# Convolution and gated FFN on one core: turning the last block's second half of results apart, slots 4, 5 and slots 6, 7, for a last transform with zero-padded tables

## Chip, cores and metric

The kernel runs on 1 core of one Trainium2 chip. The metric is the device time of one execution in microseconds (us), the median of several runs. All arithmetic of the part that changes is in fp32.

## What is computed

The input is x of 2048 positions and 512 channels. It is normalised over the channels (xn). One branch convolves every channel of xn with a kernel of 2048 terms that comes from a state-space model (A, B, C, dt, 128 states a channel), by Fourier transforms; the other is a feed-forward network on xn. The result joins both:

```python
y = irfft2(rfft2(up) * rfft2(Kp))[..., :L]     # convolution, L = 2048
s = y + xn * Dskip
h = gelu(xn @ w1 + b1)
g = silu(h @ w2 + b2)
return x + s * g
```

## The kernel before

The first 396 us or so compute the feed-forward network (its gated result goes to HBM) and the convolution kernels, interleaved by an order that is written out by hand. The rest, which the change touches, is the convolution, in `NB` = 4 blocks of 128 channels. The 2048 positions are taken as 32 x 64, so that each Fourier transform has two short steps. Engines: PE is TensorE, DVE VectorE, ACT ScalarE, POOL GpSimd, SP the queue that issues most DMAs. Each engine takes its instructions in the order in which the code issues them; the last part has no planner, so the order of the lines is the order of the work.

A block passes these steps:

- `first_dft` (the 32-step, line 879) of the signal and of the convolution kernel.
- `second_dft` (line 901): the 64-step. The 32 frequencies of the first step are done in eight **slots** of four, g = 0 to 7, as matmuls on 64x64 tiles of the array.
- `spectrum`, `product`, `combine` (lines 915 to 939): ACT copies one factor out of PSUM, DVE multiplies the two spectra and adds the products to `Y`, one tile for two slots.
- `back_dft` (line 941): the inverse of the 64-step for two slots j = 0 to 3 (slots 2j, 2j + 1), into two PSUM banks `sa`, a = 0 and 1, on the upper and the lower 64 rows of the array.
- `back_out` (line 951): copies `sa` to `Z`. `Z` has two tiles, kh = 0 for slots 0 to 3 and kh = 1 for slots 4 to 7; each holds, for each of 64 positions, the 16 frequencies' real and imaginary parts, 32 numbers.
- `turn` (line 964): DVE transposes `Z` in blocks of 32x32 to `T`, in two halves s, so that the 32 numbers come to lie on the partitions.
- `last_dft` (line 982): the inverse of the 32-step. For each of four groups w of output partitions and each of G = 4 groups g of channels, one matmul on a 32x32 tile of the array (row group g, column group w) with the table `gc[:, kh]`. kh = 0 starts the sum in PSUM and kh = 1 finishes it.
- `last_out` and, in the last block, `gated` and `added`: the result is multiplied by the gate, x is added, and `store` sends it to HBM.

An fp32 matmul shows as two passes in the trace, each with a weight load of its own (PEld), so 16 matmuls are 32 records.

In blocks 0 to 2, `two_slots` lays a block's last steps beside the next block's first ones. The last block has `slot` for its eight slots, and behind slot 7 a tail of its own (line 1197 on). There the results of slots 6, 7 (j = 3) are computed in halves h0 and h1, and the outputs in two halves of positions, `py[0]` (in two tiles `wide`) and `py[1]` (four banks). The order of the tail before: back_dft and back_out for h0, then for h1 (bank 0 copied by ACT, bank 1 by DVE); last_dft of kh = 0 on the first half; two transposes `turn(b, 1, s)` of all of kh = 1; four matmuls of an identity matrix on PE, whose result is overwritten; last_dft of kh = 0 on the second half; last_dft of kh = 1 on the first and the second half. Then come `gated` (lines 1223 and 1226) and `added` (line 1230) and four stores. `gated(0, n)` needs the first half of the outputs, `gated(1, n)` the second.

Of the kernel before, what the change touches and what calls it, by code (L numbers as in the profile page):

```python
# [11 lines left out]
F32 = mybir.dt.float32  # L12
# [8 lines left out]
P = 128  # L21
L, D, NS, F = 2048, 512, 128, 1792
G = D // P
NF = F // P
KD = D // P
N1, N2 = 32, 64
NB = 4
# [5 lines left out]
NQ = L // P  # L33
# [95 lines left out]
def _shape_constants():  # L129
    n1 = np.arange(N1)[:, None]  # L130
    k1 = np.arange(N1)[None, :]
    a = 2 * np.pi * n1 * (k1 + 0.25) / N1
    cf = np.zeros((G, N1, 2, 2, N1))
    for g in range(G):
        cf[g, :, g % 2] = np.stack([np.cos(a), -np.sin(a)], 1)
    cg = np.stack([np.cos(a).T, -np.sin(a).T], 1).reshape(2, 2, 4, 2, 2, N1)
    cg = np.tile(cg.transpose(1, 3, 2, 4, 0, 5).reshape(1, N1, 2, N1), (G, 1, 1, 1))
    n2 = np.arange(N2)[:, None]
    k2 = np.arange(N2)[None, :]
    cm = np.zeros((2, N2, N1, 2, N2))  # L140
    ct = np.zeros((2, N2, N1, 2, N2))
    for k in range(N1):
        th = 2 * np.pi * (n2 * (k + 0.25) / L + n2 * k2 / N2)
        c, s = np.cos(th), np.sin(th)
        cm[:, :, k, 0, :] = c
        cm[:, :, k, 1, :] = s
        ct[0, :, k, 0, :] = c.T / L
        ct[1, :, k, 0, :] = -s.T / L
        ct[0, :, k, 1, :] = s.T / L
        ct[1, :, k, 1, :] = c.T / L  # L150
    ct = ct.reshape(2, N2, N1 // 2, 2, 2, N2).transpose(3, 1, 2, 0, 5, 4)
    cb = np.zeros((CH, NPC, CH, NPH))
    for d in range(CH):
        cb[d, :3, d, :N1] = N2 * np.arange(N1)
        cb[d, :3, d, N1:] = np.arange(N2 // 2) + 0.5
        cb[d, 3:, d, :N1] = 1.0
    f = np.float32
    return {
        "cf": cf.reshape(P, 4 * N1).astype(f),
        "cg": cg.reshape(P, 2 * N1).astype(f),  # L160
        "cm": cm.reshape(P, N1 * 2 * N2).astype(f),
        "ct": ct.reshape(P, N1 * P).astype(f),
        "cb": cb.reshape(CH * NPC, CH * NPH).astype(ml_dtypes.bfloat16),
    }
# [3 lines left out]
def kernel(  # L168
# [5 lines left out]
    V, A, GP, PE, SY = nc.vector, nc.scalar, nc.gpsimd, nc.tensor, nc.sync  # L174
# [613 lines left out]
    def open_mid():  # L788
        SB["pm"] = pm = opened(p2, "pm", "right")
        SB["ps"] = opened(pz, "psm", "left", bufs=2, space=PSUM)  # L790
        SB["tcn"] = pm.tile([P, N1, P], F32, name="tcn")
        SB["tb"] = SB["tcn"].rearrange("p (k o) m -> p k o m", o=2)
        xf[1] = pm.tile([P, 2, 2, N1, N2], F32, tag="X1", name="X1")
        SB["uh"] = pm.tile([P, 2, 2, P], F32, tag="uh", name="uh_0_0", bufs=2)
        SB["t0"] = pm.tile([P, 2, 2, 4, N2], F32, tag="t0", name="t0_0_0", bufs=2)
        SB["gc"] = pm.tile([P, 2, N1], F32, name="gc")
        gx[0] = new_tail(0)
        yy[0, "T", 1] = new_turn(0, 1)

# [141 lines left out]
    def back_dft(b, j, es=slice(0, 4)):  # L941
        if (b, j, "p") not in yy:
            yy[b, j, "p"] = [bank(f"sa{b}_{j}_{a}") for a in range(2)]
        for e in range(4)[es]:
            for o in range(2):
                for a, p in enumerate(yy[b, j, "p"]):
                    r = slice(64 * a, 64 * a + 64)
                    PE.matmul(p[:, e, :], yy[b, j][r, o, e, :], SB["tb"][r, 4 * j + e, o, :],  # L948
                              start=(o == 0), stop=(o == 1), skip_group_check=True)

    def back_out(b, j, es=slice(0, 4), engs=(A, A)):
        kh = j // 2
        if (b, "Z", kh) not in yy:
            yy[b, "Z", kh] = SB["pm"].tile([P, N2, N1 // 2, 2], F32, tag=f"Z{kh}", name=f"Z{b}_{kh}")
        for a, (p, eng) in enumerate(zip(yy[b, j, "p"], engs)):
            k = 8 * (j % 2) + 4 * a
            src = p.rearrange("p k (x c) -> p x k c", c=2)[:, :, es]
            dst = yy[b, "Z", kh][:, :, k:k + 4, :][:, :, es]
            eng.copy(dst, src) if eng is A else eng.tensor_copy(dst, src)

    def new_turn(b, kh):
        return SB["pm"].tile([P, 4, 2, 8, N1], F32, tag=f"T{kh}", name=f"T{b}_{kh}")

    def turn(b, kh, s):
        if (b, "T", kh) not in yy:
            yy[b, "T", kh] = new_turn(b, kh)
        Z = yy[b, "Z", kh].rearrange("p (w s q) k c -> p w s q (k c)", w=4, s=2)
        V.transpose(yy[b, "T", kh][:, :, s], Z[:, :, s])

    gx = {}  # L970

# [10 lines left out]
    def last_dft(b, kh, py, q=slice(0, NQ)):  # L982
        T = yy[b, "T", kh].rearrange("p w s q i -> p w (s q) i")
        for w in range(4):
            for g in range(G):
                r, m = slice(g * N1, (g + 1) * N1), slice(w * N1, (w + 1) * N1)
                o = py[g].rearrange("p (q i) -> p q i", i=N1)
                PE.matmul(o[m], SB["gc"][r, kh], T[r, w, q], start=(kh == 0), stop=(kh == 1), skip_group_check=True)  # L988
# [173 lines left out]
    with tc.manual_schedule():  # L1162
        SB["spare"] = False
        open_front()
        z_load(NTB - 1)
        for j in range(4):
            mc_load(j)
        side_skip(0)
        side_turn(1, eng=GP)
        SB["spare"] = True  # L1170
        for p in "S0 F00 S1 S2 F01 S3 L0 F10 L1 A0 F11 A1 L2 L3 A2 A3".split():
            if p[0] == "F":
                k = int(p[1]), int(p[2])
                first_dft(0, *k)
                first_out(0, *k, (A, A, V, V))
                if k[0]:
                    mc_turn(k[1])
                    if k[1] == 0:
                        kernel_load(1)
            elif p[0] == "A":  # L1180
                silu(NTB - 1, int(p[1]))
            else:
                second_part(*steps[-2 if p[0] == "S" else -1], int(p[1]))
                if p[0] == "L":
                    z_add(NTB - 1, int(p[1]))
        z_store(NTB - 1)
        SB["spare"] = False
        fa.close()
        open_mid()
        ct_load(0)  # L1190
        SY.dma_start(SB["gc"].rearrange("p h n -> p (h n)"), cg)
        for b in range(NB - 1):
            for i in range(4):
                two_slots(b, i)
        for g in range(8):
            slot(NB - 1, g)
        b = NB - 1
        h0, h1 = slice(0, 2), slice(2, 4)
        back_dft(b, 3, h0)
        back_out(b, 3, h0)  # L1200
        wide = [SB["ps"].tile([P, 2, 4 * P], F32, tag="ri", name=f"y{b}_{n}", bufs=2) for n in range(2)]
        py = [[wide[g // 2][:, g % 2, :2 * P] for g in range(G)]]
        halves = [slice(0, NQ // 2), slice(NQ // 2, NQ)]
        back_dft(b, 3, h1)
        back_out(b, 3, h1, (A, V))
        last_dft(b, 0, py[0], halves[0])
        py.append([bank(f"y{b}_{g}_1").rearrange("p e m -> p (e m)")[:, :2 * P] for g in range(G)])
        for s in range(2):
            turn(b, 1, s)
        for n in range(4):  # L1210
            PE.matmul(py[1][0][:, :P], ident, ident, start=True, stop=True, skip_group_check=True)
        last_dft(b, 0, py[1], halves[1])
        for s in range(2):
            last_dft(b, 1, py[s], halves[s])
        gt, xt_ = gx[b]
        def parts(s, n):
            return tuple(t[:, halves[s], 64 * n:64 * n + 64] for t in (gt, xt_))

        def gated(s, n):
            if s:  # L1220
                for g in (2 * n, 2 * n + 1):
                    gg = gt[:, halves[1], g * N1:g * N1 + N1]
                    V.tensor_mul(gg, py[1][g].rearrange("p (q i) -> p q i", i=N1), gg)
            else:
                gp = parts(0, n)[0].rearrange("p q (g i) -> p g q i", i=N1)
                V.tensor_mul(gp, wide[n][:, :, :2 * P].rearrange("p g (q i) -> p g q i", i=N1), gp)

        def added(s, n):
            gv, xv = parts(s, n)
            (V if n else GP).tensor_add(xv, gv, xv)  # L1230

        gated(0, 0)
        added(0, 0)
        gated(0, 1)
        gated(1, 0)
        added(0, 1)
        for t in range(2):
            store(b, t, (SY, A)[t % 2])
        gated(1, 1)
        for n in range(2):  # L1240
            added(1, n)
        for t in range(2, 4):
            store(b, t, (SY, A)[t % 2])
# [33 lines left out]
```

## Time and profile before

| | us |
|---|---|
| median of 3 runs | 533.06 (532.49 to 534.91) |
| the profiled execution, its own time | 532.96 |
| its span from first to last instruction | 531.1 |
| PE busy in the span | 516.4 |
| DVE busy | 429.7 |
| ACT busy | 390.8 |
| POOL busy | 260.7 |

The mean granted clock of TensorE was 0.995. Times in the profile run from the span's start. A row of the order of time has start, length, engine, line, operation, what is written from what, and the count; in brackets stands how long the engine was idle before and what ended that. A row of the chain that ended last has start, length, engine, tile and line. A row of a stretch has its bounds and length and then, for each engine, the busy time and the count of instructions in it. PE names the passes, PEld the weight loads.

### The profile page before, as it was taken

Reading aid. Unit: us, or ns where it says so; the run is one execution under the profiler, and the core shown is the slowest. Engines: PE = TensorE matmul, PEld = TensorE weight load, DVE = VectorE, ACT = ScalarE, POOL = GpSimd, SP = SyncE. Lnnn points to the kernel's source line nnn. Section 1 sums busy time; section 2 is a strip of 40 time slices with the busy share of each in tenths; the row PEclk is TensorE's granted clock in tenths of the full one; section 3 lists DMA queues with packets and bytes.
Section 4 is the critical chain, followed back from the end, with each engine's and each line's share of the span. In section 5 each row is a group of like instructions: output and inputs, shape, how many; then the busy total and the mean of one; then the engine's idle time right before and its main releaser. Section 6 shows DMA issues by size and latency. Waiting matters only on the chain.

```text
span 531.1 us, 16527 instructions
## 1 busy us (share of the span) xinstructions
PE 516.4 (97%) x6999; PEld 422.4 (80%) x6999; DVE 429.7 (81%) x726; ACT 390.8 (74%) x556; POOL 260.7 (49%) x384
## 2 busy tenths in 40 slices
PE   8899999999999999999999999999999999999993
PEld 8677787877777777877777787778889998998882
DVE  6989899999998789787875886898257779677896
ACT  3588996999987988888778799799454573663330
POOL 5619478667597569669817175645301002103042
PEclk9999999999999999999999999999999999999998
DMA  7946527762427966418135532591656639542552
GB/s 221 307 121 195 187 94 233 241 199 77 161 80 198 352 215 180 140 29 252 41 108 175 185 59 107 133 176 45 233 209 224 77 102 214 164 166 81 195 193 97
DMA packets 86086, 85.84 MB, mean 162 GB/s; under 512 B 41878, under 2 KB 60698, under 8 KB 84988
## 3 DMA queue, kind: packets, MB, share of 16 engines
q1 hardware_dynamic: 76944, 66.43, 42.3%
q0 software_dynamic: 8768, 17.83, 10.8%
q8 instruction: 55, 0.90, 0.7%
q10 hardware_dynamic: 300, 0.53, 0.3%
q14 instruction: 19, 0.16, 0.1%
HBM read 51.22 MB, written 33.55 MB: 160 GB/s over the span
## 4 chain that ended last, share of the span: by engine, by line
PE 84%; DVE 6%; ACT 3%; POOL 3%; DMA 2%; issue 2%; POOLq 0%; DVEq 0%; ACTq 0%
PE s L911 11%; PE z L287 9%; PE z L289 8%; PE z L288 8%; PE f L248 8%; PE f L250 8%; PE f L249 8%; PE s L889 6%; PE sa L948 6%; PE kg L655 5%; PE ph L591 3%; PE y L988 2%; DMA w1s<-in_B_w_dram 1%; DVE hl L274 1%; PE xT L359 1%
## 5 line engine op out<-in xcount | busy, mean ns | idle before, releaser
L616 POOL TENSOR_TENSOR mm<-mm,rc 128x32 f32<-128x32 f32 (+4 forms) x150 | 97.1, 647 | 11.8
L287 PE MATMUL z<-w2h,hh 128*128 128x512 f32 x224 | 95.6, 427 | 0.0
L248 PE MATMUL f<-xh,w1h 128*128 128x512 f32 x220 | 91.7, 417 | 0.9 <-ACT w1h L231 0.6
L250 PE MATMUL f<-xh,w1l 128*128 128x512 f32 x220 | 87.1, 396 | 2.2 <-DVE w1l L233 1.5
L289 PE MATMUL z<-w2h,hl 128*128 128x512 f32 x224 | 87.7, 392 | 0.1
L288 PE MATMUL z<-w2l,hh 128*128 128x512 f32 x224 | 87.7, 391 | 0.0
L249 PE MATMUL f<-xl,w1h 128*128 128x512 f32 x220 | 86.8, 394 | 0.0
L605 DVE SCALAR_TENSOR_TENSOR ra<-ra,ph 128x512 f32<-128x512 f32 x64 | 43.8, 684 | 19.4 <-ACT ra L599 18.5
L911 PE MATMUL s<-X,mc 64*64 64x128 f32 x1536 | 58.0, 272 | 0.4 <-DVE t L929 0.4
L929 DVE TENSOR_TENSOR t<-s,uh 128x512 f32<-128x512 f32 x64 | 40.9, 684 | 15.1 <-ACT uh L919 11.6
L250 PEld LDWEIGHTS f<-xh,w1l 128*128 128x128 f32 x220 | 41.3, 188 | 12.4 <-DVE w1l L233 2.4
L639 DVE TENSOR_TENSOR e<-mm,ra 128x1024 f32<-128x1024 f32 x32 | 42.7, 1336 | 10.0 <-ACT ra L627 4.2
L248 PEld LDWEIGHTS f<-xh,w1h 128*128 128x128 f32 x220 | 41.5, 189 | 11.4 <-ACT w1h L231 1.1
L262 ACT ACTIVATE f<-f,b1s 128x512 f32<-128x512 f32 x56 | 37.2, 665 | 18.1 <-PE f L250 16.9
L289 PEld LDWEIGHTS z<-w2h,hl 128*128 128x128 f32 x224 | 42.1, 188 | 10.1 <-DVE hl L274 0.5
L613 POOL COPY mm<-rc 128x32 f32<-128x32 f32 x30 | 15.5, 516 | 69.5 <-DVE e L646 39.6
L287 PEld LDWEIGHTS z<-w2h,hh 128*128 128x128 f32 x224 | 42.4, 189 | 8.9 <-issue 0.3
L911 PEld LDWEIGHTS s<-X,mc 64*64 64x64 f32 x1536 | 44.8, 133 | 5.3 <-issue 1.5
L288 PEld LDWEIGHTS z<-w2l,hh 128*128 128x128 f32 x224 | 42.2, 189 | 8.2
L249 PEld LDWEIGHTS f<-xl,w1h 128*128 128x128 f32 x220 | 41.3, 188 | 9.1
L919 ACT COPY uh<-s 128x512 f32<-128x512 f32 x32 | 18.8, 587 | 40.1 <-PE s L911 22.0
L274 DVE TENSOR_TENSOR hl<-f,hh 128x512 fp32r<-128x512 f32 x56 | 37.8, 682 | 10.6 <-ACT hh L268 10.6
(183 smaller groups left out, 1130.9 us busy)
## 6 DMA issues: line engine op xcount, KB each, us to landing
x<-in_A_u_dram SPq DMA_DIRECT2D x8, 512.0 KB
xs<-x SPq DMA_DIRECT2D x8, 512.0 KB
xt_h<-xh POOLq DMA_DIRECT2D x4, 1024.0 KB, 5.7
xt_l<-xl POOLq DMA_DIRECT2D x4, 1024.0 KB, 8.2
kgd<-ko SPq DMA_DIRECT2D x16, 256.0 KB
za<-zo SPq DMA_DIRECT2D x4, 1024.0 KB
xh<-xt_h POOLq DMA_DIRECT2D x4, 1024.0 KB, 6.7
xl<-xt_l POOLq DMA_DIRECT2D x4, 1024.0 KB, 10.0
```

What stands on the lines that cost most here:

```text
L248: PE.matmul(p, wh[:, k, :], xh[:, k, :], start=(k == 0), stop=False)
L249: PE.matmul(p, wh[:, k, :], xl[:, k, :], start=False, stop=False)
L250: PE.matmul(p, wl[:, k, :], xh[:, k, :], start=False, stop=(k == KD - 1))
L274: V.tensor_sub(hl, hf, hh)
L287: PE.matmul(z, hh[:, s], wh, start=(f0 == 0 and not rows), stop=False)
L288: PE.matmul(z, hh[:, s], wl, start=False, stop=False)
L289: PE.matmul(z, hl[:, s], wh, start=False, stop=(f0 == FA - 1))
L605: V.scalar_tensor_tensor(ra[:, 0, c], ra[:, 1, c], MAGIC, p, op0=ALU.subtract, op1=ALU.subtract)
L616: GP.tensor_mul(mv[:, :, 0:3:2, w:2 * w], mv[:, :, 0:3:2, 0:w], rc[:, 2 + 2 * i:4 + 2 * i, :].rearrange("p j c -> p c j").unsqueeze(3).to_ ...
L639: V.tensor_mul(e1, m1.unsqueeze(1).to_broadcast([P, 2, CH, N1]), ra[:, :, :, :N1])
L911: PE.matmul(p[ka * 64:(ka + 1) * 64, r, o, :, jj], w, xf[b][h, c, :, k, :], start=(c == 0), stop=(c == 1), skip_group_check=True)
L929: V.tensor_mul(t, p[:, i, :, 1].unsqueeze(1).to_broadcast([P, 2, 2, P]), uh)
```

## The change

For kh = 1 of the last block, `back_out` writes `Z` in another layout: slots 4, 5 (j = 2, written as j % 2 = 0) fill its first half and slots 6, 7 its second, each with 64 positions by 16 numbers. A 32x32 block of a transpose then holds two neighbouring positions by 16 numbers instead of one by 32. So slots 4, 5 can be transposed (`turn_pairs(b, 0, s)`) before slots 6, 7 are there. After a transpose the partitions hold 16 numbers of the even position and 16 of the odd one. `last_pairs` therefore has two matmuls, e = 0 and e = 1, for each group pair (w, g), with tables whose other 16 rows are zeros, and each gives every second position: 128 columns instead of 256. `gc` grows from 2 to 6 tables of 32 columns.

```diff
+    pair = np.zeros((G, 2, 2, 2, N1 // 2, N1))
+    for j in range(2):
+        for o in range(2):
+            pair[:, j, o, o] = cg[:, N1 // 2 * j:N1 // 2 * (j + 1), 1]
+    pair = pair.reshape(G, 4, N1, N1).transpose(0, 2, 1, 3)
+    cg = np.concatenate([cg, pair], 2)
...
-        SB["gc"] = pm.tile([P, 2, N1], F32, name="gc")
+        SB["gc"] = pm.tile([P, 6, N1], F32, name="gc")
...
-            dst = yy[b, "Z", kh][:, :, k:k + 4, :][:, :, es]
+            if b == NB - 1 and kh:
+                Z = yy[b, "Z", kh].rearrange("p x k c -> p (x k c)").rearrange("p (j x k c) -> p j x k c", j=2, k=N1 // 4, c=2)
+                dst = Z[:, j % 2, :, 4 * a:4 * a + 4, :][:, :, es]
+            else:
+                dst = yy[b, "Z", kh][:, :, k:k + 4, :][:, :, es]
...
+    def turn_pairs(b, j, s):
+        if (b, "T", 1) not in yy:
+            yy[b, "T", 1] = new_turn(b, 1)
+        Z = yy[b, "Z", 1].rearrange("p x k c -> p (x k c)").rearrange("p (j w s q) -> p j w s q", j=2, w=4, s=2)
+        T = yy[b, "T", 1].rearrange("p w s q i -> p (w s q i)").rearrange("p (j s w q) -> p j s w q", j=2, s=2, w=4)
+        V.transpose(T[:, j, s], Z[:, j, :, s])
+
+    def last_pairs(b, j, py, s):
+        T = yy[b, "T", 1].rearrange("p w s q i -> p (w s q i)").rearrange("p (j s w q) -> p j s w q", j=2, s=2, w=4)
+        for w in range(4):
+            for g in range(G):
+                r, m = slice(g * N1, (g + 1) * N1), slice(w * N1, (w + 1) * N1)
+                o = py[g].rearrange("p (q e i) -> p q e i", e=2, i=N1)
+                for e in range(2):
+                    PE.matmul(o[m, :, e], SB["gc"][r, 2 + 2 * j + e], T[r, j, s, w], start=False, stop=(j == 1), skip_group_check=True)
...
         back_dft(b, 3, h0)
         back_out(b, 3, h0)
         wide = [SB["ps"].tile([P, 2, 4 * P], F32, tag="ri", name=f"y{b}_{n}", bufs=2) for n in range(2)]
         py = [[wide[g // 2][:, g % 2, :2 * P] for g in range(G)]]
-        halves = [slice(0, NQ // 2), slice(NQ // 2, NQ)]
+        last_dft(b, 0, py[0], halves[0])
         back_dft(b, 3, h1)
-        back_out(b, 3, h1, (A, V))
-        last_dft(b, 0, py[0], halves[0])
+        for s in range(2):
+            turn_pairs(b, 0, s)
+        back_out(b, 3, h1)
+        last_pairs(b, 0, py[0], 0)
         py.append([bank(f"y{b}_{g}_1").rearrange("p e m -> p (e m)")[:, :2 * P] for g in range(G)])
-        for s in range(2):
-            turn(b, 1, s)
-        for n in range(4):
-            PE.matmul(py[1][0][:, :P], ident, ident, start=True, stop=True, skip_group_check=True)
         last_dft(b, 0, py[1], halves[1])
         for s in range(2):
-            last_dft(b, 1, py[s], halves[s])
+            turn_pairs(b, 1, s)
+        last_pairs(b, 1, py[0], 0)
+        for j in range(2):
+            last_pairs(b, j, py[1], 1)
```

On DVE this is the tail before, from slot 7's last combination on (Y_3, Z_1 and T_1 are the tiles of slots 6, 7 and of kh = 1; T_0 and Z_0 those of kh = 0; y_0, y_1 are the first half of the outputs, y_0_1 and on the second):

```order
L937 TENSOR_TENSOR Y_3_7115<-t_3_6_7111,t_3_6_7112 128x2x128
L968 STREAM_TRANSPOSE T_0_7074<-Z_0_7061 128x4x256
L959 COPY Z_1_7175<-sa_3_1_7184 128x64x4
L968 STREAM_TRANSPOSE T_1_7227<-Z_1_7175 128x4x256 x2
L1226 TENSOR_TENSOR last<-y_0_7195,last 128x2x8x32
L1226 TENSOR_TENSOR last<-y_1_7196,last 128x2x8x32
L1223 TENSOR_TENSOR last<-y_0_1_7223,last 128x8x32
```

And the same place on DVE after the change:

```order
L943 TENSOR_TENSOR Y_3_7115<-t_3_6_7111,t_3_6_7112 128x2x128
L978 STREAM_TRANSPOSE T_0_7074<-Z_0_7061 128x4x256
L985 STREAM_TRANSPOSE T_1_7221<-Z_1_7175 128x512 x4
L1254 TENSOR_TENSOR last<-y_0_7195,last 128x2x8x32
L1254 TENSOR_TENSOR last<-y_1_7196,last 128x2x8x32
L1251 TENSOR_TENSOR last<-y_0_1_7258,last 128x8x32
```

DVE's copy has gone to ACT, and two transposes have become four of half the size, of which the first two read what slots 4, 5 left. On PE, this is the tail before, from back_dft's second half on, each kind of row once:

```order
L948 MATMUL sa_3_1_7184<-tcn,Y_3_7115 128x128
L988 MATMUL y_0_7195<-T_0_7074,gc 32x256 x2
...
L1211 MATMUL y_0_1_7223<-ident 128x128 x4
L988 MATMUL y_0_1_7223<-T_0_7074,gc 32x256
...
L988 MATMUL y_0_7195<-T_1_7227,gc 32x256 x2
...
L988 MATMUL y_0_1_7223<-T_1_7227,gc 32x256
```

And on PE after the change (in a row of 32x4x32 the four matmuls are e = 0, 1 of two channel groups, in one of 32x4x32 x2 they are e = 0, 1 of one):

```order
L1014 MATMUL y_0_7195<-T_0_7074,gc 32x256 x2
...
L954 MATMUL sa_3_1_7184<-tcn,Y_3_7115 128x128
L994 MATMUL y_0_7195<-T_1_7221,gc 32x4x32 x4
...
L1014 MATMUL y_0_1_7258<-T_0_7074,gc 32x256
...
L994 MATMUL y_0_7195<-T_1_7221,gc 32x4x32 x4
...
L994 MATMUL y_0_1_7258<-T_1_7221,gc 32x4x32 x2
```

The first half's last_dft has moved ahead of back_dft's second half, the identity matmuls are gone, and each of the two calls that read T_1 has become two calls of twice as many matmuls.

More of the change, by code (lines that the diff above doesn't have):

```diff
@@ L159, in _shape_constants @@
         "cf": cf.reshape(P, 4 * N1).astype(f),
-        "cg": cg.reshape(P, 2 * N1).astype(f),
+        "cg": cg.reshape(P, 6 * N1).astype(f),
         "cm": cm.reshape(P, N1 * 2 * N2).astype(f),
@@ L1198 @@
         h0, h1 = slice(0, 2), slice(2, 4)
+        halves = [slice(0, NQ // 2), slice(NQ // 2, NQ)]
         back_dft(b, 3, h0)
```

## The prediction

> **What bounds the kernel now.** I read the page first, then the chain that ended last from 505 us on, then the rows of the engines in order of time for the last 15 us. On the page TensorE (PE) is busy for nearly the whole span. The other three lines serve later: all instructions, and the bytes that two instruction queues fetched.
>
> ```profile
> span 531.1 us, 16527 instructions
> PE 516.4 (97%) x6999; PEld 422.4 (80%) x6999; DVE 429.7 (81%) x726; ACT 390.8 (74%) x556; POOL 260.7 (49%) x384
> ...
> q8 instruction: 55, 0.90, 0.7%
> q14 instruction: 19, 0.16, 0.1%
> ```
>
> That share says nothing of the place of the change, which lies behind slot 7 of the last block. The chain there (start, length, work) changes hands:
>
> ```profile
> 511.10 3.65 PE s L911 x128
> 514.75 2.04 PE sa L948 x32
> 516.78 1.34 ACT Z L959 x3
> 518.12 0.04 issue
> 518.17 1.43 PE sa L948 x16
> 519.60 0.64 PE y L988 x32
> 520.24 1.09 PE y L1211 x8
> 521.33 1.41 PE y L988 x59
> 522.74 0.02 issue
> 522.76 0.12 DVE last L1226
> ...
> 523.97 0.18 DVE last L1223
> ```
>
> The reader is to see that PE hands over to VectorE (DVE) at 522.76, and that DVE then carries it. What stands on both engines, and on ScalarE (ACT), in that time:
>
> ```profile
> 516.76 1.63 ACT L959 COPY Z<-sa 128x512 f32<-128x512 f32 x4 [1.32 <-PE sa L948]
> 517.73 1.24 DVE L968 STREAM_TRANSPOSE T<-Z 128x1024 f32<-128x1024 f32 x1
> 518.17 1.43 PE L948 MATMUL sa<-tcn,Y 64*128 64x128 f32 x16 [0.54 <-ACT Z L959]
> 519.43 0.37 ACT L959 COPY Z<-sa 128x256 f32<-128x256 f32 x1 [1.04 <-PE sa L948]
> 519.53 0.71 PE L988 MATMUL y<-T,gc 32*32 32x256 f32 x32
> 519.69 0.42 DVE L959 COPY Z<-sa 128x256 f32<-128x256 f32 x1 [0.72 <-issue]
> 520.22 2.37 DVE L968 STREAM_TRANSPOSE T<-Z 128x1024 f32<-128x1024 f32 x2
> 521.26 2.15 PE L988 MATMUL y<-T,gc 32*32 32x256 f32 x96
> 522.76 1.29 DVE L1226 TENSOR_TENSOR last<-y,last 128x512 f32<-128x512 f32 x2 [0.17 <-PE y L988]
> 523.97 0.74 DVE L1223 TENSOR_TENSOR last<-y,last 128x256 f32<-128x256 f32 x2
> 526.04 0.97 DVE L1230 TENSOR_TENSOR last<-last 128x512 f32<-128x512 f32 x1
> ```
>
> So today the two transposes (520.22 to 522.59) set when PE may finish, PE's last passes trail them by under a microsecond, and from 523.97 on DVE works without a gap until 527.0. The stores and the closing of the program then take the 4.1 us to 531.1, the same in either kernel. I sum against this execution: 531.1 of span plus 1.86 around it, 532.96, which is 0.1 below the median of 533.06.
>
> **The change, part by part.**
>
> *Copies.* The copy of sa_3_1's second half moves from DVE to ACT. DVE loses 0.42. ACT's own takes 0.37 (row at 519.43), two at most 0.75: to 520.2 at the latest, where DVE's copy ends at 520.1 today. ACT has nothing else to do then.
>
> *Transposes.* Two of 128x1024 become four of 128x512:
>
> ```profile
> L968 DVE STREAM_TRANSPOSE T<-Z 128x1024 f32<-128x1024 f32 x3 | 3.6, 1228 | 0.1
> ```
>
> No row shows a 512-wide one. By elements it is half of 1.23, 0.62; the bound above is the 0.69 of a 512-wide product. Four take 2.46 to 2.8; I take 2.46. The two of slots 4, 5 need only ACT's copies of before 518.4 and run from 518.97 (end of the transpose in the second row) to 520.2, where DVE now stands idle for 0.72 and copies. The other two run from about 520.3 to 521.55. The transposes thus end 1.0 earlier than today's 522.59.
>
> *The last transform of slots 0 to 3, first half,* moves ahead of back_dft's second half: 0.71 of PE (row at 519.53) into the gap of 0.54 ahead of 518.17, in which PE waits for ACT's copies (third row). That leaves 0.2 over for a step that ends at 519.60; I take 0.1, since only one of its two row halves is released as early as that. If the cover went, it would cost 0.71. The four identity matmuls (1.09) go; they filled PE's wait for the transposes, so nothing is gained.
>
> *The last transform of slots 4 to 7* is the real price. Two calls of 16 matmuls over 256 columns become four calls of 32 matmuls over 128 columns: 8,192 columns become 16,384, since half of each padded table is zeros, and the two matmuls e = 0 and e = 1 stand one behind the other **on the same 32x32 tile**. An fp32 matmul is two passes, each with its load (16 matmuls are the x32 of the row at 519.53). One pass of 128 columns occupies a tile for 3.65/32 = 0.114 us: the chain's 128 passes at 511.10 go round four 64x64 tiles, 32 on each. So a tile needs 4 x 0.114 = 0.46 per call. What a call costs depends on how many tiles PE keeps going. The trace shows this in the transform of the block before, 16 matmuls with table half 0 and 16 with half 1, in five stretches (length, then busy time and count of PE and of its loads); below them one row of the loads in order of time, and two of the groups by tile:
>
> ```profile
> 503.05:503.30 0.25, 0.23 (x16) 0.23 (x32) 0.00 (x0) 1.00 0.93 98
> 503.30:503.50 0.20, 0.20 (x16) 0.00 (x0) 0.00 (x0) 1.00 0.42 82
> 503.50:503.64 0.14, 0.14 (x32) 0.10 (x1) 0.00 (x0) 1.00 0.80 263
> 504.06:504.14 0.08, 0.08 (x17) 0.00 (x0) 0.00 (x0) 1.00 1.09 410
> 504.14:504.30 0.16, 0.16 (x22) 0.16 (x18) 0.00 (x0) 1.00 1.41 474
> ...
> 503.52 0.10 PEld L988 LDWEIGHTS y<-T,gc 32*32 32x32 f32 x1 [0.22 <-issue]
> ...
> L988 PE MATMUL y<-T,gc x320: 374/587/612, 444.5 to 523.0; 32*32 32x512 f32 x96, 32*32 32x256 f32 x64
> L1191 SPq DMA_DIRECT2D gc<-in_cg_dram x1: 333/333/333, 396.2 to 396.2; - x1
> ```
>
> All 32 loads and the 16 first passes of sixteen matmuls start in the first stretch, none in the second, and the second passes in the third. One load follows at 503.52, with the first second pass; no other runs at 504.06 to 504.14, and then they come in numbers. The row below has the median pass of the group, 0.587: begun at 503.52, the first second pass ends at 504.11, just before the loads return. My reading: PE holds sixteen matmuls, and takes the next as the oldest is *finished*. In the new order sixteen matmuls are eight tiles, so a call is two fills. A fill is four passes on a tile, 0.46, and then the end of a pass, which is later than its turn:
>
> ```profile
> L911 PE MATMUL s<-X,mc 64*64 64x128 f32 x1536 | 58.0, 272 | 0.4 <-DVE t L929 0.4
> ```
>
> 0.27 - 0.11 = 0.16 more, 0.62 a fill, **1.24 a call**. A call on 256 columns costs (522.74 - 521.26)/2 = 0.74.
>
> *Where the sum lands.* From back_dft's end, 519.7 with the 0.1: first new call 1.24, old call 0.74, new call 1.24, gives 522.9 for the first half of the outputs (522.74 today; its last transpose ended at 520.9, so that doesn't hold it). Two more calls, 2.48, end at 525.4. DVE starts the first product at 522.9, is through two at 524.2, and waits for PE until about 525.3 (it needs groups 0, 1 only), where the row today reads 523.97: **+1.3**. Behind that wait on DVE stand the addition for the first two stores, and all else up to the end; it moves along as a block. 532.96 + 1.3 = **534.3**, 1.2 above the median.
>
> The larger table (96 instead of 32 KB) is loaded at 396.2, 48 us before its first use at 444.5: nothing.
>
> **The rivals.**
>
> *All sixteen tiles go.* If the limit of sixteen matmuls isn't one, a call is 0.46 + 0.16 and up to 0.2 over which sixteen passes start (all in the first stretch above), of which I take 0.1: 0.72. Then the first half of the outputs is ready at 519.7 + 0.72 + 0.74 + 0.72 = 521.9, DVE's products run to 523.2, PE ends at 523.3: 0.7 before 523.97, **532.3**. The sum turns where 519.7 + 0.74 + 4X is 523.97, at X = 0.88 a call. For: two passes per tile were overtaken freely. Against: the empty stretch.
>
> *A tile's queue is short.* If what waits for a tile may only be a few instructions deep, the next tile starts once the second pass of a tile's first matmul has begun: 0.114 and a load of 0.03, 0.14 x 16 = 2.3 a call. PE ends at 519.7 + 0.74 + 9.2 = 529.6, +5.5: **538.5**. For: no row of the profile shows two matmuls in a row on one tile. Against: on four tiles (511.10) PE keeps a steady 0.114, with the next matmul's load and passes waiting behind those of the last.
>
> *Matmuls start in order.* If the second matmul of a tile must begin before the next tile's first, a tile holds all others for two passes and a load, 0.25: 4.0 a call, 16.0 in all, PE ends at 536.4, +12: **545**. This is the case that makes the kernel slower beyond doubt; it decides from X = 1.56 a call, where the loss passes 2.7.
>
> [...] Taken for single passes it would let each of the 16 matmuls at 519.53 begin only with the second pass of the one before, 2 x 0.114 later: 16 x 0.23 = 3.6, where the trace has 0.71 and, in the block before, sixteen first passes ahead of any second. The passes are instructions of their own: 0.90 MB / 13,998 PE and load records is 64 bytes each, as 0.16 MB / 2,529 is for the other engines. So the trace does not agree for passes; for whole matmuls no row tells, and this rival keeps its chance.
>
> **How the numbers follow.** Sixteen in flight, 534.3: 0.62, within 533.8 to 535.3 by the bounds of its terms (0 to 0.7 for the moved call, of which 0.1 is taken; 0.1 either way for each new call). All tiles, 532.3: 0.12. Short queue, 538.5: 0.15. In order, 545: 0.11. To hold 8 in 10 the range takes in the first three cases: 532.0 to 538.9. Over or under 0.5% (2.7 us, about what a measurement of this kernel tells from no change): faster 0.01, same 0.73, slower 0.26.
>
> **What would show it.** In the new profile: four DVE transposes of about 0.62, the first at 518.97; back_dft's second half ending by 519.8; calls of the padded tables 1.2 long, with loads pausing twice in each; the first product on DVE at 522.9 and the third at 525.3 with an idle time before it that PE ended. A call under 0.9 means that the window is wider; one of 2.3 or 4.0 means one of the slower cases. Transposes much dearer than 0.7 would make DVE the bound and the PE sum moot.

## The result, and the profile after

The changed kernel takes 536.34 us (median of 9 runs, 535.29 to 537.97), the kernel before 534.08 beside it (9 runs, 532.49 to 534.91). The medians lie 2.3 us apart; the ratio is 1.0053, 95% interval 1.0038 to 1.0068, which of 534 us is 2.8 (2.0 to 3.6). So the change makes the kernel some 0.5% slower. The forecast was slower by 1.3, and 536.34 lies in its range; by the medians the price is 1.0 larger than the sum made it.

The profiled execution took 537.65 (span 535.9, granted clock 0.997). These are the lines of the page that answer to those that the prediction shows of before:

```profile
span 535.9 us, 16896 instructions
PE 520.3 (97%) x7183; PEld 426.3 (80%) x7183; DVE 430.0 (80%) x727; ACT 390.8 (73%) x557; POOL 259.6 (48%) x384
...
q8 instruction: 56, 0.92, 0.7%
q14 instruction: 20, 0.16, 0.1%
```

PE has 184 passes and as many loads more (6,999 before), and one packet of instructions more. VectorE (DVE) and ScalarE (ACT) in order of time, from the transpose of T_0 on:

```profile
520.22 1.24 DVE L978 STREAM_TRANSPOSE T<-Z 128x1024 f32<-128x1024 f32 x1
521.38 2.53 DVE L985 STREAM_TRANSPOSE T<-Z 128x512 f32<-128x512 f32 x4
521.93 0.65 ACT L969 COPY Z<-sa 128x256 f32<-128x256 f32 x2 [1.04 <-PE sa L954]
525.64 1.29 DVE L1254 TENSOR_TENSOR last<-y,last 128x512 f32<-128x512 f32 x2 [1.73 <-PE y L994]
...
528.74 0.79 DVE L1251 TENSOR_TENSOR last<-y,last 128x256 f32<-128x256 f32 x2 [1.81 <-PE y L994]
...
530.82 0.97 DVE L1258 TENSOR_TENSOR last<-last 128x512 f32<-128x512 f32 x1
```

DVE now waits for PE ahead of the first product and again, 1.81, ahead of the third. The chain that ended last shows the same from PE's side:

```profile
520.12 0.67 PE y L1014 x32
520.79 1.30 PE sa L954 x16
522.10 0.01 issue
522.11 1.15 PE y L994 x45
...
524.25 2.19 PE y L994 x94
526.44 0.70 issue
527.13 1.58 PE y L994 x69
528.71 0.02 issue
528.74 0.42 DVE last L1251
```

The line to see is "526.44 0.70 issue": in the midst of the last calls, PE stands idle and waits for nothing that the profile shows. The loads, in order of time, have the same stop, 0.96 long there:

```profile
523.77 2.40 PEld L994 LDWEIGHTS y<-T,gc 32*32 32x32 f32 x106
527.13 1.72 PEld L994 LDWEIGHTS y<-T,gc 32*32 32x32 f32 x84 [0.96 <-issue]
```

Two executions can't be compared from their start here. PE also stops much earlier, in parts that the change leaves alone; two such rows of the loads of the changed kernel:

```profile
448.03 0.30 PEld L917 LDWEIGHTS s<-X,mc 64*64 64x64 f32 x9 [1.40 <-issue]
...
453.07 1.08 PEld L895 LDWEIGHTS s<-fc,in 64*128 64x128 f32 x18 [1.10 <-issue]
```

The profiled execution of before has neither, and 1.40 + 1.10 = 2.5 is about how much later the changed kernel's T_0 transpose starts (520.22 against 517.73). Other profiled executions have shorter stops at these places, one or two, or none (the hybrid below); with the medians 2.3 apart and the profiled executions 4.7, that part is read as no effect of the change. So all that follows counts from **the start of that transpose**, T_0's:

| start after T_0's transpose | first product | third product | last operation of DVE |
|---|---|---|---|
| before | 522.76 - 517.73 = 5.03 | 523.97 - 517.73 = 6.24 | 526.04 - 517.73 = 8.31 |
| after | 525.64 - 520.22 = 5.42 | 528.74 - 520.22 = 8.52 | 530.82 - 520.22 = 10.60 |

The tail ends 10.60 - 8.31 = 2.29 later, as much as the medians differ. Of it 2.28 are there at the third product.

### The profile page after: what moved, and what is told of

The parts are those of the page before. It is cut to its first block, busy times and chain, and to the rows that moved or that the text cites. A ratio compares the mean times of both kernels' runs of the same rounds, so it can differ in the third digit from the quotient of the medians.

```text
span 535.9 us, 16896 instructions
## 1 busy us (share of the span) xinstructions
PE 520.3 (97%) x7183; PEld 426.3 (80%) x7183; DVE 430.0 (80%) x727; ACT 390.8 (73%) x557; POOL 259.6 (48%) x384
## 4 chain that ended last, share of the span: by engine, by line
PE 86%; DVE 8%; DMA 2%; issue 2%; ACT 1%; ACTq 0%; DVEq 0%
PE s L917 11%; PE z L293 9%; PE z L295 9%; PE z L294 9%; PE f L254 8%; PE f L256 8%; PE f L255 8%; PE s L895 6%; PE sa L954 6%; PE kg L661 5%; PE ph L597 3%; PE y L1014 2%; PE xT L365 1%; PE y L994 1%; DMA w1s<-in_B_w_dram 1%
## 5 line engine op out<-in xcount | busy, mean ns | idle before, releaser
L917 PEld LDWEIGHTS s<-X,mc 64*64 64x64 f32 x1536 | 45.9, 133 | 6.9 <-issue 2.9
```

What stands on the lines that cost most here:

```text
L917: PE.matmul(p[ka * 64:(ka + 1) * 64, r, o, :, jj], w, xf[b][h, c, :, k, :], start=(c == 0), stop=(c == 1), skip_group_check=True)
```

## The experiments

**Theory A**: the calls cost what the forecast says (sixteen matmuls in flight, so eight tiles a fill), and the 0.96 is PE's own instructions coming late: they arrive in blocks, and behind back_dft PE now has 4 x 32 + 16 matmuls of two passes and two loads each, 576 short instructions in a row. **B**: the doubled columns of the padded tables are the price. **C**: the idle time belongs to a place in the tail, not to the supply. **D**: the new order or ACT's copies cost. **E**: transposes or copies are dearer than forecast.

### The moved step alone

The kernel before, with the first half of kh = 0 moved and both copies on ACT; no padded tables.

```diff
+        last_dft(b, 0, py[0], halves[0])
         back_dft(b, 3, h1)
-        back_out(b, 3, h1, (A, V))
-        last_dft(b, 0, py[0], halves[0])
+        back_out(b, 3, h1)
```

> The kernel before, with only the order of the change: last_dft of kh = 0 on the first half ahead of back_dft's second half, and both copies of that half on ACT; layout, transposes, last transform and identity matmuls stay. Measured from the start of the last 1024-wide transpose of T_0 on DVE, the third product (written from y_0_1) stands at 6.24 us before and at 8.52 in the changed kernel. Theory A (the extra matmuls of the padded tables and the fetching of their instructions are the whole loss): 6.1 to 6.3 here, ratio to the kernel before 0.998 to 1.002. Rival D (the order or ACT's second copy costs part of it): 6.5 to 7.0, ratio 1.001 to 1.002.

533.23 us, ratio 0.9994 (0.9972 to 1.0016). DVE, from T_0's transpose on:

```profile
518.63 1.24 DVE L968 STREAM_TRANSPOSE T<-Z 128x1024 f32<-128x1024 f32 x1
520.98 2.37 DVE L968 STREAM_TRANSPOSE T<-Z 128x1024 f32<-128x1024 f32 x2 [1.11 <-ACT Z L959]
523.27 1.25 DVE L1226 TENSOR_TENSOR last<-y,last 128x512 f32<-128x512 f32 x2
524.45 0.74 DVE L1223 TENSOR_TENSOR last<-y,last 128x256 f32<-128x256 f32 x2
```

The third product is at 524.45 - 518.63 = 5.82, under all that was expected: the order and the copies cost nothing, they give 0.4 in the tail, since the products now stand directly behind the transposes. D falls.

### The two matmuls of a pair sixteen apart

The changed kernel with the loop over e outermost in `last_pairs`, so that sixteen matmuls in a row are on sixteen tiles.

```diff
-        for w in range(4):
-            for g in range(G):
-                r, m = slice(g * N1, (g + 1) * N1), slice(w * N1, (w + 1) * N1)
-                o = py[g].rearrange("p (q e i) -> p q e i", e=2, i=N1)
-                for e in range(2):
+        for e in range(2):
+            for w in range(4):
+                for g in range(G):
+                    r, m = slice(g * N1, (g + 1) * N1), slice(w * N1, (w + 1) * N1)
+                    o = py[g].rearrange("p (q e i) -> p q e i", e=2, i=N1)
```

> The changed kernel with the loop over e outermost in last_pairs, so that sixteen matmuls in a row go to sixteen tiles. Same work, same number of instructions. Theory A (PE holds sixteen matmuls at a time, in the changed kernel on eight tiles; and PE's instructions come in blocks of 256, a block of which cannot be used up in under 3.5 us): a call of a padded table takes 0.85 instead of 1.3, the first product stands at 4.5 instead of 5.42 from the T_0 transpose; the idle time of PE in the third or fourth call stays or grows, to 1.0 to 2.0, so the third product comes at 6.8 to 7.4 instead of 8.52; about 1.3 us faster than the changed kernel, still 0.5 to 1.2 slower than before. Rival B (the doubled columns set the time, whatever the order): first product 5.3 to 5.5, third 8.3 to 8.6. Rival C (the idle time is no limit of the fetch): third product at 6.2, the kernel equal to the one before.

535.38 us, ratio 1.0033 (1.0012 to 1.0053). DVE, from T_0's transpose on:

```profile
516.64 1.24 DVE L978 STREAM_TRANSPOSE T<-Z 128x1024 f32<-128x1024 f32 x1
...
522.00 1.29 DVE L1254 TENSOR_TENSOR last<-y,last 128x512 f32<-128x512 f32 x2 [1.70 <-PE y L994]
525.24 0.76 DVE L1251 TENSOR_TENSOR last<-y,last 128x256 f32<-128x256 f32 x2 [1.95 <-PE y L994]
```

The first product is at 522.00 - 516.64 = 5.36 and the third at 525.24 - 516.64 = 8.60. A had 4.5 and at most 7.4: both times lie where rival B had put them (5.3 to 5.5, 8.3 to 8.6), so by the products alone this experiment speaks for B. The loads, in order of time, show another reason:

```profile
518.52 0.78 PEld L994 LDWEIGHTS y<-T,gc 32*32 32x32 f32 x63 [0.23 <-DVE T L985]
...
520.39 0.18 PEld L1014 LDWEIGHTS y<-T,gc 32*32 32x32 f32 x17 [0.82 <-issue]
...
523.86 1.12 PEld L994 LDWEIGHTS y<-T,gc 32*32 32x32 f32 x84 [1.57 <-issue]
```

The first call's loads go out in 0.78, where those of the changed kernel take over 1.1 (522.11 to past 523.20). So the call is shorter, as A says, but PE stops twice, 0.82 + 1.57 = 2.39; A had one stop, of 1.0 to 2.0. Without the first stop the first product would stand at 5.36 - 0.82 = 4.54, and without both the third at 8.60 - 2.39 = 6.21, as good as before with all the doubled columns in it. That is worked out; whether B or the stops are the reason, the split kernel below decides. From one stop to the next there are 128 loads, which with their passes are 256 instructions, and behind the last stop are 84, as many as in the changed kernel. What the order wins, the stops take back.

### Half of the padded matmuls

Only e = 0: the odd positions' share of slots 4 to 7 is left out.

```diff
-                for e in range(2):
+                for e in range(1):
```

> The changed kernel with e = 0 alone in last_pairs: it leaves out the odd positions' share of slots 4 to 7, and with it half of the extra matmuls. Theory A: a call is 0.45, the block of 256 instructions that ran dry is not reached, the third product stands at 4.9 to 5.1 from the T_0 transpose (8.52 in the changed kernel, 6.24 before), and the kernel is 1.0 to 1.4 us faster than the one before. Rival E (transposes of 128x512, or the copies in the new layout, are dearer and hold DVE): third product at 6.0 or later, no gain.

533.57 us, ratio 1.0000 (0.9979 to 1.0022). The tail is as A had it, without a stop; DVE's rows of T_0's transpose and of the third product:

```profile
518.26 1.24 DVE L978 STREAM_TRANSPOSE T<-Z 128x1024 f32<-128x1024 f32 x1
...
523.25 0.74 DVE L1251 TENSOR_TENSOR last<-y,last 128x256 f32<-128x256 f32 x2
```

So the third product is at 4.99. The time of the whole kernel didn't follow by the 1.2 that this is under before's 6.24. Its runs spread from 530.68 to 535.26, and the profiled one has stops far ahead of the tail; the expected gain in time was not seen, and this experiment tells by its tail alone.

### Sixty-four PE instructions more at the start

Eight of the 25 matmuls that run on PE before the work begins are replaced by 24 tiny ones. That is 16 matmuls more, and with two passes and two loads each 64 PE instructions more, some 500 us ahead of an unchanged tail.

```diff
-        warm(25)
+        warm(17)
+        tiny = ps1.tile([P, P], F32, tag="f1", name="tiny", bufs=2)
+        for _ in range(24):
+            PE.matmul(tiny[:32, :1], ident[:32, :32], ident[:32, :1], start=True, stop=True, skip_group_check=True)
```

> The changed kernel with 64 more PE instructions early on (8 of the 25 first identity matmuls are replaced by 24 tiny ones; 16 matmuls more, four instructions each), so that every later block of 256 instructions ends 64 instructions earlier in the program. In the changed kernel PE stands idle for 0.96 us with 172 instructions to go. Theory A (the idle time lies at the end of a fetched block): the idle time has moved to 236 instructions before the end, is 0.8 to 1.3 long, and the end comes no earlier. Rival C (it belongs to the place in the program, or to the transfers that run then): it stays at 172 to go, or is gone.

534.08 us, in the one execution there is. The stop in the tail, in the loads:

```profile
520.71 1.64 PEld L997 LDWEIGHTS y<-T,gc 32*32 32x32 f32 x75
522.99 2.34 PEld L997 LDWEIGHTS y<-T,gc 32*32 32x32 f32 x116 [0.64 <-issue]
```

Now 116 loads stand behind it, 32 more than 84; with their passes that is 64, exactly what was put in 500 us earlier. C falls: the stop sits at a count of PE instructions, not at a place in the work. It is 0.64 long, under the 0.8 to 1.3 expected, and the tail ended 0.65 earlier than in the changed kernel (last operation at 527.24 - 517.29 = 9.95), which was not expected either.

### As many instructions, no padded tables

The decisive one: the moved step alone, with each kh = 1 call in four sweeps of sixteen matmuls over 64 columns. That is the number of matmuls of the changed kernel, and the columns of the kernel before.

```diff
-            last_dft(b, 1, py[s], halves[s])
+            for c in range(4):
+                k = halves[s].start + c * NQ // 8
+                last_dft(b, 1, [p[:, c * 2 * P // 4:(c + 1) * 2 * P // 4] for p in py[s]], slice(k, k + NQ // 8))
```

> The kernel before with the moved step (as e1_moved), its two kh = 1 calls split into four matmuls of 64 columns each, the four sweeps over the sixteen tiles one behind the other: 128 matmuls instead of 32, as many as in the changed kernel, but the plain tables and the 8,192 columns of before, each computed once. Distances are from the start of DVE's last 1024-wide transpose. Theory A (PE's instructions come in blocks of 256, and a block can't be used up in under 3.0 to 3.5 us): the split calls cross a block's end some 190 instructions before the program's PE work ends, with an idle time of 1 to 2 us that PE's issue ended, and the third product starts at 7.2 to 8.3 (5.82 in e1_moved, 8.52 in the changed kernel); time 1.4 to 2.5 over e1_moved. Theory B (the doubled columns of the padded tables are the price): no such idle time, third product at 6.0 to 6.5, time within 0.7 of e1_moved. The first product comes at 4.9 to 5.2 by both.

535.26 us, ratio 1.0043 (1.0019 to 1.0067), and 2.0 over the moved step alone (533.23; the kernel before took 533.11 and 533.19 beside the two). PE's loads in order of time, and then DVE's products:

```profile
521.23 1.71 PEld L988 LDWEIGHTS y<-T,gc 32*32 32x32 f32 x164 [0.56 <-DVE T L968]
525.14 0.97 PEld L988 LDWEIGHTS y<-T,gc 32*32 32x32 f32 x92 [2.21 <-issue]
```

```profile
517.55 1.24 DVE L968 STREAM_TRANSPOSE T<-Z 128x1024 f32<-128x1024 f32 x1
...
522.71 1.29 DVE L1228 TENSOR_TENSOR last<-y,last 128x512 f32<-128x512 f32 x2 [0.41 <-PE y L988]
526.26 0.76 DVE L1225 TENSOR_TENSOR last<-y,last 128x256 f32<-128x256 f32 x2 [2.26 <-PE y L988]
```

No column is computed twice, and yet the third product is at 526.26 - 517.55 = 8.71, later than in the changed kernel, behind a stop of 2.21. A's range ended at 8.3, B's at 6.5: the mechanism is A's, the stop was even longer. B falls as the reason for the idle time.

### The hybrid: padded tables for the first half of the positions alone

The new layout and copies, and `last_pairs` with e outermost for the first half; for the second half of the positions kh = 1 is transposed whole, by four transposes of 128x256 (`turn_whole`), and goes through one plain call of sixteen matmuls (`last_whole`). The order of the tail:

```diff
-        for s in range(2):
-            turn_pairs(b, 0, s)
+        turn_pairs(b, 0, 0)
         back_out(b, 3, h1)
         last_pairs(b, 0, py[0], 0)
...
+        turn_pairs(b, 1, 0)
+        turn_whole(b)
+        last_pairs(b, 1, py[0], 0)
         last_dft(b, 0, py[1], halves[1])
-        for s in range(2):
-            turn_pairs(b, 1, s)
-        last_pairs(b, 1, py[0], 0)
-        for j in range(2):
-            last_pairs(b, j, py[1], 1)
+        last_whole(b, py[1])
```

> The changed layout and copies, but padded tables (e loop outermost) for the first half of the positions alone; the second half of kh = 1 is transposed whole out of the new layout by four 128x256 transposes and goes through one plain call of sixteen matmuls with 256 columns. PE has 384 passes and loads instead of 580 behind back_dft's second half. Theory A: only one block's end falls into the tail, reached after a block that PE took over 4 us for, so no idle time or one under 0.4; third product at 5.5 to 5.9 (6.24 in the kernel before), time 0 to 1.0 under the kernel before, ratio 0.998 to 1.001. Theory B (the padded columns are the price, 1.7 or more for two calls): third product at 6.5 or later, time 0.3 to 1.5 over the kernel before.

532.43 us (12 runs, 531.68 to 534.21), ratio 0.9988 (0.9971 to 1.0004). DVE:

```profile
517.91 1.24 DVE L978 STREAM_TRANSPOSE T<-Z 128x1024 f32<-128x1024 f32 x1
...
520.92 1.38 DVE L991 STREAM_TRANSPOSE T<-Z 128x256 f32<-128x256 f32 x4
522.23 1.25 DVE L1265 TENSOR_TENSOR last<-y,last 128x512 f32<-128x512 f32 x2
523.40 0.75 DVE L1262 TENSOR_TENSOR last<-y,last 128x256 f32<-128x256 f32 x2
```

First product at 4.32, third at 523.40 - 517.91 = 5.49, with no wait for PE and no stop in the tail: 0.75 better than before there. Against the kernel before the interval holds no change, so it is the best tail found but no proven gain; against the changed kernel it is the better one.

### The moved step without the identity matmuls

```diff
-        for n in range(4):
-            PE.matmul(py[1][0][:, :P], ident, ident, start=True, stop=True, skip_group_check=True)
```

> As e1_moved without the four identity matmuls, the cheapest form of the moved step. Theory A (and the prediction's step that the identity matmuls fill a wait): third product at 5.8 to 6.1, time within 0.6 of the kernel before, ratio 0.998 to 1.001. A rival, that PE's clock or the next call suffers where PE stands idle: granted clock under 0.98 behind the gap, third product at 6.5 or later, time 0.4 to 1.0 over the kernel before.

533.96 us, ratio 1.0009 (0.9988 to 1.0031); third product at 525.79 - 519.94 = 5.85, granted clock 0.995. In the tail the identity matmuls filled a wait and nothing more (5.82 with them). The median is 0.85 over the kernel before's 533.11, where at most 0.6 was expected; the interval holds no change.

### One count for all stops

The counts of the pages, put beside the loads behind the tail's stop, give one place in the program. These are the pages' lines of the kernel with e outermost, of the shifted one, of the split one and of the one with half of the tables padded:

```profile
PE 517.0 (97%) x7183; PEld 423.2 (79%) x7183; DVE 428.8 (81%) x727; ACT 390.7 (73%) x557; POOL 258.6 (49%) x384
```

```profile
PE 519.3 (98%) x7215; PEld 425.5 (80%) x7215; DVE 429.5 (81%) x727; ACT 391.0 (73%) x557; POOL 260.9 (49%) x384
```

```profile
PE 517.9 (97%) x7191; PEld 423.6 (79%) x7191; DVE 429.1 (80%) x725; ACT 391.0 (73%) x557; POOL 260.3 (49%) x384
```

```profile
PE 516.4 (97%) x7087; PEld 422.7 (80%) x7087; DVE 429.3 (81%) x729; ACT 390.7 (74%) x557; POOL 259.1 (49%) x384
```

| kernel | loads in all | behind the stop | ahead of it |
|---|---|---|---|
| after | 7183 | 84 | 7099 |
| e outermost | 7183 | 84 | 7099 |
| shifted by 64 instructions | 7215 | 116 | 7099 |
| split, plain tables | 7191 | 92 | 7099 |
| half padded; before | 7087; 6999 | none | never reached |

Four kernels, with three different tails, stop at the same load of PE's program, and two that end ahead of it have no such stop in the tail. One packet of q8 is 0.92 MB / 56 = 16.4 KB, which at 64 bytes an instruction (the prediction's 0.90 MB / 13,998) is 256, the distance of the two stops in the second experiment.

The stops far ahead of the tail fit the same count. In the changed kernel, 5,060 loads have started before the stop at 448.03 and 5,187 before that at 453.07. With as many passes, and with PE's semaphore instructions, which the trace holds too, these places lie 4,095 and 3,840 instructions ahead of load 7,099: sixteen and fifteen blocks of 256, to within one. Four other profiled executions stop at load 5,187 as well, for 0.26 to 0.83 us, and seven, the kernel before among them, at load 5,825, ten blocks ahead of 7,099, for 0.27 to 0.78.

So the stops fit the ends of blocks of 256 instructions, but not every end has one. The four kernels that reach load 7,099 stop there for 0.64 to 2.21 us; the kernel before stops for 0.27 at load 5,825 and not at loads 5,060 and 5,187.

## Why the prediction was right in its sign and short in its size

- **Copies, transposes, the moved step.** As forecast: four transposes in 2.53 (2.46 taken), two copies in 0.65, back_dft's second half over 1.88 after T_0's transpose started (522.10 - 520.22), where the forecast had 519.6 - 517.73 = 1.87 and 0.1 more. Moved alone, they even give 0.4 (first experiment). E falls with them.
- **Sixteen in flight, eight tiles a fill.** Right in kind. In the first padded call, stretches of 0.2 from 522.05 on (busy time and count of PE, then of its loads) show the pause that the prediction named as the sign, loads in number, few, and then many again, though once in the call and not twice:

```profile
522.05:522.30 0.25, 0.19 (x12) 0.19 (x21) 0.00 (x0) 1.00 0.00 0
522.30:522.50 0.20, 0.20 (x28) 0.20 (x24) 0.00 (x0) 1.00 0.00 0
522.50:522.70 0.20, 0.20 (x28) 0.19 (x8) 0.00 (x0) 1.00 0.00 0
522.70:522.90 0.20, 0.20 (x18) 0.19 (x10) 0.00 (x0) 1.00 0.00 0
522.90:523.10 0.20, 0.20 (x22) 0.20 (x26) 0.00 (x0) 1.00 0.00 0
```

  The first three calls took 522.11 to 525.64, 3.5 against 1.24 + 0.74 + 1.24 = 3.22. With the loop turned (second experiment) the first call is shorter (its loads take 0.78 against over 1.1), as it must be if eight tiles were the limit. Sixteen matmuls have 32 loads, and the trace nearly agrees: 34 loads start up to 522.47, before the pause.
- **The rivals.** Matmuls in order (4.0 a call) and the short queue (2.3) would have made three calls 8.7 and 5.3, where 3.5 was measured; they fall. All tiles at once (0.72 a call, so 2.2 for three) falls with the pause. That matmuls don't start in order is seen directly, too: in the changed kernel the first passes of the old call (L1014) start before the last of the padded call's 64 (L994), which stands ahead of it in the program:

```profile
523.00 0.40 PE L1014 MATMUL y<-T,gc 32*32 32x256 f32 x1
...
523.32 0.27 PE L994 MATMUL y<-T,gc 32*32 32x128 f32 x1
```

- **The sum on PE: the step that failed.** "Two more calls, 2.48, end at 525.4", and the third product at "about 525.3", 525.3 - 517.73 = 7.57 after T_0's transpose. Measured: 8.52, of which 0.96 is the stop of the loads, so 7.56 without it (the passes stood idle for 0.70, which would leave 7.82). The calls were right together, but that they were so to 0.01 is luck, since two errors cancel (the first three 0.3 too cheap; the last two, 528.74 - 0.96 - 525.64 = 2.14 up to the third product against 525.3 - 522.9 = 2.4, about as much too dear); **PE's supply of instructions was missing from the sum**. The prediction had the row: it used q8's bytes to count instructions and didn't ask how fast they come. In the kernel before the answer costs nothing in the tail: it ends at load 6,999, 100 loads ahead of the place. With 184 loads and as many passes more, the changed kernel needs the next block of 256, and sooner than it is there. That the time lies in the range is luck in part: 536.34 is above the 533.8 to 535.3 that the prediction gave its own case, and the range reached further only because it took in the short queue, which falls.
- **The price of the columns.** If the stops only delay what is behind them, the doubled columns cost 0.4 (6.21 in the second experiment, 5.82 in the first), the order of the two matmuls on one tile 1.35 (7.56 against 6.21), and the supply 0.96. That split is worked out, not shown: with so many instructions, every order that was run ended behind a stop, at 8.52, 8.60 and 8.71.
- **No gain on the other side.** Turning slots 4, 5 early ended the transposes 523.91 - 520.22 = 3.69 after T_0's transpose started (521.38 + 2.53), against 522.59 - 517.73 = 4.86 before: 1.17 earlier (forecast 1.0). DVE then stands idle for 1.73. The gain was made, and PE's longer work took it back at once.

Left open: how PE's supply works in between. The profile's view of DMA shows two q8 packets between 522.2 and 530 in the changed kernel, one for each block that began there. In the second experiment the block from stop to stop took 523.86 - 520.39 = 3.47. The block ahead of it held PE up too, though it had lasted longer: 128 loads back from the stop at 520.39 lie 76 of the two calls, back_dft's 16, the moved step's 32 and four more ahead of those, so it began before the moved step (516.45) and had lasted over 3.9. So a fixed time per block doesn't explain both stops. The times of the packets come closer. In the second experiment one q8 packet starts at 517.97 and one at 521.48, and the two stops end 2.42 and 2.38 after them; the stops at load 7,099 in the changed kernel, the shifted and the split one end 2.43, 2.40 and 2.68 after the packets at 524.70, 520.59 and 522.46. So in the tail a stop ends 2.4 to 2.7 us behind the start of a packet, and what differs more is how long a packet starts after the stop or the block's first instruction: 1.09 after the stop at 520.39, and 1.5 or more after the moved step at 516.45, while the DMA engines were busy with the stores of the block before (384 GB/s from 516 to 518; a share of 0.47 of the 4.36 from 516.02 to 520.38, so 2.05 us of all of them). That busy DMA engines delay a packet fits this but wasn't tried, and why the stops near 448 and 453 come in some executions only isn't settled.

## What to carry to other kernels

When an edit turns few long matmuls into many short ones, count PE's instructions too, loads and passes apart, and compare with the densest stretch that the kernel already runs; an "issue" idle time at the same count of loads in several kernels (here load 7,099 in four) is the sign that the supply has become the bound. Pairs of matmuls on one tile are better kept as far apart as there are tiles: the first call's loads went out in 0.78 us instead of over 1.1, although here the supply took the gain back. And a transpose started early is worth only what the engine that reads it has to spare: here PE, not DVE, had become last, and the 1.17 gained stood beside 1.73 of DVE waiting for PE.

## What the runs showed of the hardware that was not expected

- PE's loads stopped in the tail for 0.64, 0.82, 0.96, 1.57 and 2.21 us with nothing to wait for, always at load 7,099 or 128 loads ahead of it, and each stop ended 2.4 to 2.7 us after the start of a q8 packet.
- From one stop's end to the next one's, a block of 256 instructions took 3.47 us (1.57 of it the stop), some 13.6 ns each.
- Passes of a later call start before the last passes of the call ahead of it (523.00 against 523.32 in the changed kernel).
- Executions of one kernel differ by 2.4 to 5.5 us (534.0 to 537.8 for the split kernel) at granted clocks of 0.993 to 0.998. The profiled ones differ in their stops at blocks' ends; that these are a part of the difference is likely but not shown, since the profiled execution of the kernel with half of the padded matmuls has two that before's has not (0.90 at 411, 0.65 at 451) and is under its own median (532.26 against 533.57).
